# The small tasks of both batch halves in one slot between the large matmuls

## The chip, the cores and the metric

One NeuronCore of a Trainium2 chip runs one program. The metric is the device time of that program in microseconds; less is better. The kernel before takes 1516.54 us (median of three runs, 1514.53 to 1518.94).

## The reference

Three stages follow one another. Batch 4, 8 heads, 768 positions, head width 48; 3072 tokens of width 384.

```python
k_n = k / (norm(k) + 1e-06)                    # delta rule, one position after another
for t in range(S):
    y[t] = q[t] @ state
    v_old = state.T @ k_n[t]
    state = state + beta[t] * outer(k_n[t], v[t] - v_old)
p = domain_probs / (domain_probs.sum(-1) + 1e-09)
x1 = sum over 4 experts e of p[:, e] * (relu(x @ w1[e]) @ w2[e])      # 384 -> 1024 -> 384
out = (sigmoid(x1 @ w_gate) * (x1 @ w_val)) @ w_out                   # 384 -> 1536 -> 384
```

## The kernel before, in words

The delta rule is cut into 12 steps of 64 positions (`c` from 0 to 11). Within a step it becomes small matmuls and one triangular system per head, which VectorE solves by forward substitution ("inv"). Two steps give a block of 512 tokens, and the two MLP stages work on a block at a time. Each phase is one expert of one block (`m1`, 8 units) or the second MLP of one block (`m2`, 12 units). The first block's first expert is two phases of 256 tokens. In each unit `emit_a` (L689) makes the hidden part `ph` and `emit_b` (L726) multiplies it back into `acc`. Each product of float32 numbers is three passes over split operands (`xhi`, `xlo`, `hhi`, `hlo`, and the weights `ws`), so a large matmul has 512 columns and comes in threes. After `emit_a`, VectorE and ScalarE split the new hidden part; `emit_b` uses it two units later, and at the end of a phase all at once. At the end of the last expert's phase `finish` makes `xhi` and `xlo` of the second MLP out of `acc`, through VectorE and ScalarE.

The delta rule's work is laid between the large matmuls. The batch's four sequences sit two and two on the partitions, and `i` (0 or 1) says which half of the batch a task is for. `chain(c)` lists the rows of a step in the order of their dependence, each with a task for `i = 0` and one for `i = 1`:

- `ks` (`ks_task`, L499 and L500): keys times state into `pk`; VectorE then writes `R` = `V` - `pk`
- `half` (`half_task`, L512, steps 0 to 3 alone): two halves of the triangular solve; after the first ScalarE writes `U`, after the second VectorE writes `R`
- `tb` (`tb_task`, L521): the solved inverse `Xbd` times `R` into `pu`; VectorE writes `rhsA` and `rhsB`
- `y` (`y_task`, L534 and L535, for early steps L546): the outputs; ScalarE copies them out
- `s` (`s_task`, L571 and L572): the new state; ScalarE copies it into `rhsA` and `rhsB`

A `tb` or `half` task shows as 16 matmuls in the trace; `ks`, `y` and `s` as 32, 16 for each of their two lines. `plan_g` plans four Gram tasks a step (`g_task`, L318, 8 matmuls each in the trace), two heads' groups `hg` for each half `i`. The results of a task go into a PSUM bank of `at_p`, which has two.

The order of all this is written out by a planner when the program is built. `plan(t, fn, kind)` puts an item on the list `todo` with a planned time, in microseconds of large matmuls alone. The main loop counts such time in `now`, and calls `slot()` at fixed places: after each `emit_a`, after each `emit_b`, and inside each `emit_a` of the second MLP. A slot issues the items that are due, up to and with the first one of kind "pe". So one "pe" item goes into one slot. A step's rows lie `gap` apart (1.9 for step 1, 3.9 from step 2 on), and slots are about 1.94 apart (0.98 in the phases of 256 tokens). Work of VectorE that has time (the substitution, and the decoding of the second MLP's weights) is issued by `fill()` at these places. It goes by two counters: `pe_at`, the time that PE's work so far should have taken, and `vec_at` for VectorE. `fill` stops adding when `vec_at` is more than `SLACK` ahead of `pe_at`.

Of the kernel before, what the change touches and what calls it, by code (L numbers as in the profile page):

```python
# [84 lines left out]
def moe_delta_kernel(  # L85
# [17 lines left out]
    pe_at, vec_at = [0.0], [0.0]  # L103
# [176 lines left out]
    q = [nc.sync, None]  # L280

    def load_kq(c):
        (q[1] or q[0]).dma_start(out=KQ, in_=kq[c])

    def load_ks(c):
        (q[1] or q[0]).dma_start(out=KS, in_=kq[c, :, 0])

    def fill_bd(bd, t, i, eng):
        eng(out=bd[64:112, i, :, 0:C], in_=t[i][64:112, 0])
        eng(out=bd[0:48, i, :, C:P], in_=t[i][0:48, 0])  # L290

    def load_ys(c):
        if c:
            (q[1] or q[0]).dma_start(out=YQ[64:112, 0], in_=kq[c, 64:112, 1])
            (q[1] or q[0]).dma_start(out=YQ[0:C, 1], in_=kq[c, 0:C, 1])
        kv = kt[c].rearrange("p (i h d) -> p i h d", i=2, h=H)
        (q[1] or q[0]).dma_start(out=KI[0:C, 0], in_=kv[0:C])
        (q[1] or q[0]).dma_start(out=KI[C:P, 1], in_=kv[C:P])
        pd = pd_t.pop(c).rearrange("p (i h t) -> p i h t", i=2, h=H)
        q[0].dma_start(out=YQ[0:C, 0], in_=pd[0:C])  # L300
        q[0].dma_start(out=YQ[C:P, 1], in_=pd[C:P])

    def load_v(c):
        (q[1] or q[0]).dma_start(out=V.rearrange("p i h d -> p (i h d)"), in_=vt[c])
# [9 lines left out]
    def g_mm(i, hg, bd, kq_t):  # L314
        pg = bank([P, 4, 2, C], "pg")
        for j in range(4):
            h = hg * 4 + j
            nc.tensor.matmul(out=pg[:, j], lhsT=bd[0:112, i, h], rhs=kq_t[i][0:112, :, h], start=True, stop=True)  # L318
        return pg

    def g_l(pg, c, i, hg):
        hs = slice(hg * 4, hg * 4 + 4)
        vec.tensor_tensor(
            out=Lts[c % 2][:, i, hs],
            in0=pg[:, :, 0],
            in1=w_all[:, 2 * c + i, hs].unsqueeze(2).to_broadcast([P, 4, C]),
            op=ALU.mult,
        )

    def g_p(pg, c, i, hg):  # L330
        vec.tensor_tensor(
            out=Pts[c % 2][:, i, hg * 4 : hg * 4 + 4],
            in0=pg[:, :, 1],
            in1=mask_sb.unsqueeze(1).to_broadcast([P, 4, C]),
            op=ALU.mult,
        )
# [15 lines left out]
    def l_out(c):  # L352
        lt = Lts[c % 2]
        r, c2 = INV_OF[c]
        steps, small = INV[r]
        l_done.add(c)
        lv = [lt[o : o + HC].rearrange("p i h t -> p (i h) t") for o in range(0, P, HC)]
        if small:
            if c2 == 0:
                ld_t[r] = dr.tile([len(steps), 2, 2, H, 2, HC, HC], F32, tag=f"ls{len(steps)}", name="ls")  # L360
                od_t[r] = dr.tile([len(steps), 2, H, 2, HC, HC], F32, tag=f"lo{len(steps)}", name="lo")
            for a in range(2):
                for bp in range(2):
                    q[0].dma_start(
                        out=ld_t[r][c2, a, :, :, bp].rearrange("i h s t -> s (i h) t"),
                        in_=lv[2 * bp + a][:, :, a * HC : (a + 1) * HC],
                    )
            return
        if c2 == 0:
            ld_t[r] = dr.tile([len(steps), 2, H, 2, HC, 3 * HC], F32, tag="ld", name="ld")  # L370
        for bp in range(2):
            ld = ld_t[r][c2, :, :, bp]
            q[0].dma_start(out=ld[:, :, :, 0:C].rearrange("i h s t -> s (i h) t"), in_=lv[2 * bp])  # L373
            q[0].dma_start(
                out=ld[:, :, :, C:].rearrange("i h s t -> s (i h) t"), in_=lv[2 * bp + 1][:, :, HC:]
            )

    def l_off(c):
        lt = Lts[c % 2]
        r, c2 = INV_OF[c]  # L380
        if INV[r][1]:
            for bp in range(2):
                q[0].dma_start(
                    out=od_t[r][c2, :, :, bp].rearrange("i h s t -> s (i h) t"),
                    in_=lt[bp * C : bp * C + HC].rearrange("p i h t -> p (i h) t")[:, :, HC:],
                )

    def p_out(c):
        pd_t[c] = dr.tile([P, 2 * H * C], F32, tag=f"pd{c % 2}", name="pd")
        q[0].dma_start(out=pd_t[c], in_=Pts[c % 2].rearrange("p i h t -> p (i h t)"))  # L390
# [81 lines left out]
    def x_in(c):  # L472
        r, c2 = INV_OF[c]
        for bp in range(2):
            if INV[r][1]:
                for a in range(2):
                    put(Xbd, bp * C + a * HC, bp * C + a * HC, HC, xd_t[r][c2, a, :, :, bp])
            else:
                put(Xbd, bp * C, bp * C, C, xd_t[r][c2, :, :, bp])

    def off_in(c):
        r, c2 = INV_OF[c]
        if INV[r][1]:
            for bp in range(2):
                put(Ld, bp * C, bp * C + HC, HC, od_t[r][c2, :, :, bp])

    def scale_v(c):
        for i in range(2):
            nc.gpsimd.tensor_tensor(
                out=R[:, i] if c == 0 else V[:, i],  # L490
                in0=V[:, i],
                in1=nrm_all[:, 2 * c + i].unsqueeze(2).to_broadcast([P, H, D]),
                op=ALU.mult,
            )
# [100 lines left out]
    def chain(c):  # L595
        rows = [[lambda i=i: ks_task(c, i) for i in range(2)]] if c else []
        if INV[INV_OF[c][0]][1]:
            rows += [[lambda i=i, q=q: half_task(c, i, q) for i in range(2)] for q in range(2)]
        rows += [[lambda i=i: tb_task(c, i) for i in range(2)]]
        if c:  # L600
            rows += [[lambda i=i: y_task(c, i) for i in range(2)]]
            rows += [[lambda i=i: s_task(c, i) for i in range(2)]] if c < NC - 1 else []
        return rows
# [170 lines left out]
    def plan(t, fn, kind=""):  # L774
        todo.append((t, len(todo), kind, fn))
# [5 lines left out]
    def fill():  # L781
        while True:
            due = sorted((v[0][0], k) for k, v in back.items() if v and v[0][0] <= now[0])
            due = [(t, k) for t, k in due if len(back[k][0]) == 3 or back[k][0][3]()]
            now_ = [k for _, k in due if back[k][0][1] != "dve"]
            if not due or not now_ and vec_at[0] > pe_at[0] + SLACK:
                return
            ks = now_ or [k for _, k in due if k != turn_[0]] or [due[0][1]]
            if ks[0] == turn_[0] == "inv":
                vec_at[0] += SERIAL  # L790
            turn_[0] = ks[0]
            back[ks[0]].pop(0)[2]()

    def slot():
        fill()
        while todo and todo[0][0] <= now[0]:
            kind = todo[0][2]
            todo.pop(0)[3]()
            if kind == "pe":
                pe_at[0] += 1.7  # L800
                break
        fill()

# [27 lines left out]
    def plan_chain(c, t, gap):  # L831
        rows = chain(c)
        if c > 1:
            plan(t - 6.0, lambda: scale_v(c))
        if c > 1 and c % 2 == 0:

            def first():
                while inv_done[0] <= INV_OF[c][0]:
                    back["inv"].pop(0)[2]()
                x_in(c)  # L840
                off_in(c)

            plan(t - 8.0, first)
        for r, row in enumerate(rows):
            for q, fn in enumerate(row):
                plan(t + gap * (r + 0.5 * q), fn, "pe")
        t1 = t + gap * len(rows)
        if c % 2 == 0 and c:
            plan(t1 - 2 * gap, lambda: (x_in(c + 1), off_in(c + 1)))
        if c + 1 < NC:  # L850
            plan(t + 2 * gap, lambda: (load_v(c + 1), load_ks(c + 1)))
            plan(t1 + 3.0 if c > 1 else 75.0, lambda: load_ys(c + 1))
        return t1
# [9 lines left out]
    def plan_g(c, t):  # L863
        plan(t, lambda: load_kq(c))
        for i in range(2):
            plan(t + 12, lambda i=i: fill_bd(bdG, KQi, i, nc.scalar.copy))

        def g_task(i, hg):
            pg = g_mm(i, hg, bdG, KQi)
            g_l(pg, c, i, hg)  # L870
            g_p(pg, c, i, hg)

        for n, (i, hg) in enumerate([(0, 0), (0, 1), (1, 0), (1, 1)]):
            plan(t + 14 + 2 * n, lambda i=i, hg=hg: g_task(i, hg), "pe")
        plan(t + 23, lambda: (l_out(c), l_off(c), p_out(c)))

    def startup():
# [146 lines left out]
    with tc.manual_schedule():  # L1024
# [11 lines left out]
        for c in range(4, NC, 2):  # L1036
            t = dec_mem[c // 2] if c < NC - 2 else dec_mem[2]
# [121 lines left out]
```

## Time and profile before

| | us |
|---|---|
| median of three runs | 1516.54 (1514.53 to 1518.94) |
| profiled execution, its own time | 1512.61 |
| its span | 1510.8 |
| PE matmul busy | 1468.1 (97%) |
| PE weight load busy | 1222.8 (81%) |
| VectorE busy | 1066.9 (71%) |
| ScalarE busy | 574.4 (38%) |
| GpSimd busy | 264.9 (18%) |

Of the chain of work that ended last, PE has 86%, VectorE 8% and DMA 3%. Busy times overlap; a matmul's end is modelled and reaches into the next one, so distances are taken from start to start.

### The profile page before, as it was taken

What the parts mean: (1) busy time and instruction counts of PE and PEld (TensorE: products, weight loads), DVE (VectorE), ACT (ScalarE), POOL (GpSimd) and SP (SyncE); (2) the same over time, 40 slices, a digit from 0 to 9 for tenths busy, and PEclk for the clock granted to TensorE, in tenths of its full rate; (3) what the DMA queues carried; (4) which work ended last, traced back from release to release, by engine and by line L of the source; (5) the groups of instructions that cost most, each with busy time, mean ns of one, the idle gap of its engine ahead of it and who ended that gap; (6) DMA issues with size and microseconds to landing.
All of it is one profiled execution on the core that took longest, in us unless ns stands there. A gap on an engine that the chain in (4) does not pass through costs nothing.

```text
span 1510.8 us, 23046 instructions
## 1 busy us (share of the span) xinstructions
PE 1468.1 (97%) x8801; PEld 1222.8 (81%) x8801; DVE 1066.9 (71%) x1905; ACT 574.4 (38%) x921; POOL 264.9 (18%) x293
## 2 busy tenths in 40 slices
PE   5799899999999999999999999999999999999998
PEld 5688777888888888888888888888888888888887
DVE  8877998846888766778766778757778754444553
ACT  4045444533333334333343333343433343433343
POOL 4241457530011200012110002220001210001000
PEclk8689999999999999999999999999999999999999
DMA  8586688675443675444584435495433463333221
GB/s 231 163 260 208 222 267 266 215 202 151 150 139 109 181 189 146 140 141 128 162 208 133 133 116 165 132 225 144 133 102 106 132 163 94 123 101 108 88 94 63
DMA packets 97749, 235.50 MB, mean 156 GB/s; under 512 B 23544, under 2 KB 29816, under 8 KB 95608
## 3 DMA queue, kind: packets, MB, share of 16 engines
q1 hardware_dynamic: 87352, 195.04, 43.2%
q0 software_dynamic: 10144, 38.94, 9.9%
q8 instruction: 69, 1.13, 0.3%
q14 instruction: 40, 0.33, 0.1%
q10 hardware_dynamic: 144, 0.07, 0.0%
HBM read 202.10 MB, written 27.97 MB: 152 GB/s over the span
## 4 chain that ended last, share of the span: by engine, by line
PE 86%; DVE 8%; DMA 3%; issue 2%; ACT 1%; SPq 0%; DVEq 0%; ACTq 0%
PE ph L689 43%; PE acc L726 33%; PE pu L521 3%; PE pg L318 2%; DVE Xpp L112 1%; DVE itmp L112 1%; PE pk L499 1%; PE ps L571 1%; DMA raw<-in_wp 1%; DVE ws L112 1%; DMA ls<-LP 1%; PE yt L534 1%; DVE hlo L112 1%; PE pu L512 1%; PE yt L535 1%
## 5 line engine op out<-in xcount | busy, mean ns | idle before, releaser
L689 PE MATMUL ph<-xhi,ws 128*128 128x512 f32 (+1 forms) x2064 | 635.4, 390 | 1.5 <-ACT xhi L756 0.8
L726 PE MATMUL acc<-hhi,ws 128*128 128x512 f32 (+1 forms) x1632 | 497.2, 387 | 0.0
L689 PEld LDWEIGHTS ph<-xhi,ws 128*128 128x128 f32 x2064 | 378.4, 188 | 77.2 <-ACT xhi L589 1.3
L689 PE MATMUL ph<-xlo,ws 128*128 128x512 f32 (+1 forms) x1032 | 398.2, 386 | 0.7 <-DVE xlo L112 0.7
L726 PEld LDWEIGHTS acc<-hhi,ws 128*128 128x128 f32 x1632 | 302.0, 189 | 59.3 <-ACT hhi L696 0.3
L112 DVE TENSOR_TENSOR ws<-raw,ws 128x768 fp32r<-128x768 f32 x308 | 298.3, 970 | 60.8 <-ACT ws L190 58.1
L726 PE MATMUL acc<-hlo,ws 128*128 128x512 f32 (+1 forms) x816 | 314.5, 385 | 8.3 <-DVE hlo L112 8.2
L190 ACT CAST ws<-raw 128x768 fp32r<-128x768 f32 x308 | 253.8, 830 | 83.5 <-PE acc L726 63.8
L696 ACT ACTIVATE hhi<-ph 128x512 fp32r<-128x512 f32 (+1 forms) x200 | 116.2, 581 | 418.6 <-PE ph L689 410.9
L689 PEld LDWEIGHTS ph<-xlo,ws 128*128 128x128 f32 x1032 | 194.2, 188 | 41.8 <-DVE xlo L112 2.6
L112 DVE SCALAR_TENSOR_TENSOR hlo<-ph,hhi 128x512 fp32r<-128x512 f32 (+1 forms) x200 | 132.6, 666 | 130.6 <-ACT hhi L696 130.5
L726 PEld LDWEIGHTS acc<-hlo,ws 128*128 128x128 f32 x816 | 154.0, 189 | 40.6 <-DVE hlo L112 10.2
L112 DVE TENSOR_TENSOR itmp<-Xpp,Lpp 128x120 f32<-128x120 f32 (+27 forms) x403 | 174.3, 445 | 9.7 <-DMA Lpp<-ls 3.8
L112 DVE TENSOR_TENSOR Xpp<-Xpp,itmp 128x120 f32<-128x120 f32 (+27 forms) x403 | 176.2, 449 | 5.1
L112 DVE TENSOR_TENSOR gv<-ph,sg 128x512 f32<-128x512 f32 x72 | 49.7, 691 | 94.7 <-PE ph L689 94.6
L705 ACT CAST hhi<-gv 128x512 fp32r<-128x512 f32 x72 | 44.6, 620 | 171.7 <-DVE gv L112 171.7
L753 POOL TENSOR_TENSOR ACC<-ACC,ctmp 128x512 f32<-128x512 f32 x36 | 50.1, 1393 | 321.1 <-DVE ctmp L112 320.5
L112 DVE TENSOR_TENSOR hlo<-gv,hhi 128x512 fp32r<-128x512 f32 x72 | 51.3, 713 | 49.4 <-ACT hhi L705 49.4
L703 ACT ACTIVATE sg<-ph 128x512 f32<-128x512 f32 x72 | 43.0, 597 | 76.7 <-PE ph L689 76.7
L373 POOL DMA_DIRECT2D ld<-LP x16 | 10.7, 670 | 333.5 <-DVE LP L112 333.5
L318 PE MATMUL pg<-KQ,bdG 112*128 112x128 f32 x320 | 45.2, 291 | 15.1 <-ACT bdG L290 10.8
L318 PEld LDWEIGHTS pg<-KQ,bdG 112*128 112x128 f32 x320 | 43.6, 205 | 20.0 <-ACT bdG L290 12.4
(163 smaller groups left out, 1104.7 us busy)
## 6 DMA issues: line engine op xcount, KB each, us to landing
raw<-in_wp SPq DMA_DIRECT2D x200, 384.0 KB, 3.1
raw<-w_d SPq DMA_DIRECT2D x108, 384.0 KB, 3.5
KQ<-in_kq SPq DMA_DIRECT2D x9, 896.0 KB, 7.9
pd<-LP POOLq DMA_DIRECT2D x12, 512.0 KB, 8.1
YQ<-pd POOLq DMA_DIRECT2D x24, 256.0 KB, 7.0
Lpp<-ld POOLq DMA_DIRECT2D x8, 768.0 KB, 13.5
pe<-p_d SPq DMA_DIRECT2D x23, 256.0 KB, 4.4
dec_a<-in_wp SPq DMA_DIRECT2D x15, 384.0 KB, 4.3
```

What stands on the lines that cost most here:

```text
L112: return fn(*args, **kw)
L190: nc.scalar.copy(out=w[:, 0], in_=t)
L318: nc.tensor.matmul(out=pg[:, j], lhsT=bd[0:112, i, h], rhs=kq_t[i][0:112, :, h], start=True, stop=True)
L499: nc.tensor.matmul(out=pk[0:C, h], lhsT=KS[C:112, i, h], rhs=rhsA[C:112, i, h], start=True, stop=True)
L512: nc.tensor.matmul(out=pu[0:m, h], lhsT=lhsT, rhs=rhs, start=True, stop=True)
L521: nc.tensor.matmul(out=pu[:, h], lhsT=Xbd[:, i, h], rhs=R[:, i, h], start=True, stop=True)
L689: nc.tensor.matmul(out=res[q], lhsT=lt, rhs=rt, start=(k == 0 and j == 0), stop=(k == KT - 1 and j == 2))
L696: nc.scalar.activation(out=hh, in_=res[0], func=AF.Relu)
L703: nc.scalar.activation(out=sg, in_=res[0], func=AF.Sigmoid)
L705: nc.scalar.copy(out=hh, in_=gv)
L726: nc.tensor.matmul(out=acc_t[d][:, :w], lhsT=lt, rhs=rt, start=(u == 0 and j == 0), stop=(u == nf - 1 and j == 2),)
L753: (nc.vector if e == NE - 1 else nc.gpsimd).tensor_tensor(out=a, in0=a, in1=t, op=ALU.add)
```

## The change

`plan_chain` plans one "pe" item for a whole row, which calls the tasks of both halves one after the other; before, the second was an item of its own, half a gap later. `plan_g` plans two items a step, each with the two Gram tasks of one half, 4 apart; before, there were four, 2 apart. In `slot` every "pe" item now adds 3.4 to `pe_at`, not 1.7. This holds as well for the four items that remain single tasks: `s` of step 0 and the transposes of step 1, two each.

```diff
             if kind == "pe":
-                pe_at[0] += 1.7
+                pe_at[0] += 3.4
                 break
...
         for r, row in enumerate(rows):
-            for q, fn in enumerate(row):
-                plan(t + gap * (r + 0.5 * q), fn, "pe")
+            plan(t + gap * r, lambda row=row: [fn() for fn in row], "pe")
...
-        for n, (i, hg) in enumerate([(0, 0), (0, 1), (1, 0), (1, 1)]):
-            plan(t + 14 + 2 * n, lambda i=i, hg=hg: g_task(i, hg), "pe")
+        for i in range(2):
+            plan(t + 14 + 4 * i, lambda i=i: [g_task(i, hg) for hg in range(2)], "pe")
```

## Rows read from the trace of the kernel before

**Rows 1.** The page, slices of the span: granted TensorE clock in tenths
```profile
PEclk8689999999999999999999999999999999999999
```
**Rows 2.** Stretches, PE alone: stretch, its length, PE busy (count), PEclk, DMA share, GB/s
```profile
49.70:80.40 30.70, 26.56 (x167) 0.50 0.61 191
107.70:118.00 10.30, 10.30 (x66) 0.50 0.90 304
186.30:189.70 3.40, 3.40 (x9) 0.51 0.98 340
300.00:1430.00 1130.00, 1130.00 (x6707) 1.00 0.50 142
```
**Rows 3.** Timeline of PE: start, us, line, out<-in, count, [idle before, releaser]
```profile
185.55 0.50 PE L726 MATMUL acc<-hlo,ws 128*128 128x512 f32 x1 [4.25 <-DVE hlo L112]
...
228.59 0.50 PE L726 MATMUL acc<-hlo,ws 128*128 128x512 f32 x1 [2.24 <-DVE hlo L112]
```
**Rows 4.** Timeline of PE around an s task and a ks task
```profile
534.68 0.39 PE L689 MATMUL ph<-xlo,ws 128*128 128x512 f32 x1
535.00 0.24 PE L571 MATMUL ps<-rhsA,KI 112*48 112x48 f32 x1
...
536.42 0.40 PE L726 MATMUL acc<-hlo,ws 128*128 128x512 f32 x1
...
537.11 0.39 PE L726 MATMUL acc<-hlo,ws 128*128 128x512 f32 x1
...
747.29 0.39 PE L726 MATMUL acc<-hlo,ws 128*128 128x512 f32 x1
...
749.24 0.40 PE L689 MATMUL ph<-xlo,ws 128*128 128x512 f32 x1
```
**Rows 5.** Timeline of PE around a Gram task and a tb task
```profile
429.31 0.40 PE L726 MATMUL acc<-hlo,ws 128*128 128x512 f32 x1
...
430.91 0.39 PE L689 MATMUL ph<-xlo,ws 128*128 128x512 f32 x1
...
520.18 0.39 PE L689 MATMUL ph<-xlo,ws 128*128 128x512 f32 x1
...
522.66 0.40 PE L689 MATMUL ph<-xlo,ws 128*128 128x512 f32 x1
```
**Rows 6.** Timeline of PE in the startup: two half tasks side by side
```profile
51.36 5.33 PE L512 MATMUL pu<-R,Xbd 128*96 128x48 f32 x32 [4.64 <-POOL LP L345]
```
**Rows 7.** Groups of PE instructions by line: count | busy us, mean ns | idle before
```profile
L499 PE MATMUL pk<-rhsA,KS 48*64 48x48 f32 x352 | 24.8, 220 | 0.0
L534 PE MATMUL yt<-YQ,rhsA 112*64 112x64 f32 x320 | 21.3, 229 | 0.0
L571 PE MATMUL ps<-rhsA,KI 112*48 112x48 f32 x352 | 20.2, 210 | 0.0
```
**Rows 8.** Timeline: start of ks, then VectorE's R, at steps 2, 6, 10
```profile
266.18 0.25 PE L499 MATMUL pk<-rhsA,KS 48*64 48x48 f32 x1
272.91 0.55 DVE L112 TENSOR_TENSOR R<-V,pk 128x384 f32<-128x384 f32 x1
...
747.61 0.25 PE L499 MATMUL pk<-rhsA,KS 48*64 48x48 f32 x1
753.34 0.55 DVE L112 TENSOR_TENSOR R<-V,pk 128x384 f32<-128x384 f32 x1
...
1207.85 0.25 PE L499 MATMUL pk<-rhsA,KS 48*64 48x48 f32 x1
1212.93 0.55 DVE L112 TENSOR_TENSOR R<-V,pk 128x384 f32<-128x384 f32 x1
```
**Rows 9.** Waits of PE after 129.4: us in total, times, longest
```profile
PE pu L512 <- DVE R L112: 0.6, 1, 0.6
```
**Rows 10.** Timeline in the first phase: VectorE's R for half, PE's wait before tb
```profile
92.96 1.00 DVE L112 TENSOR_TENSOR R<-V,pk 128x384 f32<-128x384 f32 x2
106.73 2.75 PE L521 MATMUL pu<-R,Xbd 128*128 128x48 f32 x16 [2.32 <-DVE R L112]
```

## The prediction

> **What bounds the kernel now.** I read the page's clock line first. TensorE runs at its lower level only in a few stretches of the first 190 us and at full clock from there to the end [rows 1, 2]. The stretch table then shows PE busy for 1130.00 of the 1130 us from 300 to 1430 [rows 2]. In that stretch a microsecond of PE work removed is a microsecond of the kernel, and any new wait of PE is added in full. Before 245 us it is otherwise: VectorE's queue is behind, and PE waits for it twice at the end of a phase, 4.25 us before 185.55 and 2.24 us before 228.59 [rows 3]. There PE time saved is mostly given back. What a small task costs PE beyond its own matmuls is read from the timeline around one visit, and how late VectorE answers from its timeline.
>
> **The change part by part.**
>
> *Joining two tasks in a slot.* The last large matmul before an `s` task starts at 534.68, the third one after it at 536.42: 1.74 us [rows 4]. Three large matmuls in a row take 0.69 us (536.42 to 537.11), so a visit costs 1.05 us. Inside the task a pair of matmuls comes every 0.045 us, and 16 pairs are 0.72 us. The other 0.33 us is the price of going into the task and out of it. For `ks` the same sum is 749.24 - 747.29 - 0.69 = 1.26 us against 16 pairs of 0.058 us, again 0.33 us [rows 4]. `y`, of the same build, is taken at 0.33 us too. For `tb` it is different: 522.66 - 520.18 - 0.69 = 1.79 us, and its 16 matmuls need about 0.11 us each, so almost nothing is lost at the edges [rows 5]. A Gram task (`pg`) is the same: 430.91 - 429.31 - 0.69 = 0.91 us for 8 matmuls of 0.11 us [rows 5]. I cost joining `tb`, both kinds of `half` and `pg` at zero.
>
> Does a second task join on without a gap? The trace has one such place. In the startup two `half` tasks stand side by side as one piece of 32 in 5.33 us, at half clock [rows 6], which leaves no room for a break. So a joined pair saves the whole 0.33 us; bounds 0 (each task pays its edge as now) and 0.36. The counts of L499, L571 and L534 [rows 7], divided by 16, are 22 `ks`, 22 `s` and 20 `y` tasks: 11 pairs of `ks`, 10 of `s` (the two of step 0 stay apart), 10 of `y` and one in the older form. Of these 32 pairs three fall into the first phase, below. 29 x 0.33 = 9.6 us less.
>
> The row shows an edge. The Trainium skill ("TensorE: Matmul & The Clock Gate", Part 2, step by step) says the opposite: PE pulls weight loads ahead of matmuls in flight, so that the next weights load under the running matmul. By that rule alone an edge would cost nothing and joining would save 0 instead of 9.6 us. For `tb` and `pg` the trace agrees (0.0 us); for `ks` and `s` it measures 0.33 us, and I go by the rows.
>
> *Earlier tasks wait at the start of an even chain.* Adding up the planned times, I get the same slots for the first task of nearly every row. But `ks` of steps 2, 4, 6, 8, 10 stands at the end of an expert phase, and the next row came two slots later, after 18 large matmuls and the second `ks`. Now it comes in the slot inside the first `emit_a` of the second MLP, after 12. From the first `ks` matmul that is two tasks of 0.93 us, 0.25 us of way out and 12 x 0.23 us: 4.9 us. The row needs `R`, which VectorE writes only after the finishing work of the phase in its queue, at a time that does not depend on the slots. At step 6 `ks` starts at 747.61, PE is ready at 752.5, and `R` is done at 753.34 + 0.55 + 0.06 = 753.95: a wait of 1.4 us. At step 10 it is 1212.7 against 1213.54, 0.8 us [rows 8]; steps 4 and 8, read the same way, give 0.4 and 0.9. At step 2 it is 271.1 against 273.5, 2.4 us, of which 0.6 us is waited for already [rows 8, 9]. Together 0.4 + 1.4 + 0.9 + 0.8 + 1.8 = 5.3 us more. Behind a waiting `tb` stand only the six large matmuls of that `emit_a`; nothing else is due sooner. Bounds: 0 if VectorE reaches `R` earlier, 9 if all five wait as step 2 does.
>
> Odd chains have at least nine large matmuls between dependent rows, over 3 us from a first task's end to the row that needs it. The PSUM banks alternate as before. The evacuations of a pair are queued together, so the second one's comes earlier than today. I cost this at nothing.
>
> *The first phase (82.5 to 129.4 us).* Chain 1 has one row per 1.9 us of plan. Today its 16 tasks do not fit the 14 slots, and `tb` waits 2.32 us for `R`, which stands in VectorE's queue behind the norms of steps 4 to 11 [rows 10]. With pairs the second `half` row is issued two slots earlier, ahead of the norms, so this wait goes (-2.3). In its place the first `half` row comes 1.4 us before `R` (written at 92.96 [rows 10]), and `y` about 1.4 us before the `rhs` products that now stand behind the norms (+2.8). Three pairs save 1.0; one task fewer hangs over into the next phase (-0.4). The half-clock stretch from 107.7 [rows 2] followed the wait of `tb` and cost about 4.3 us; I give two chances in three that it goes (-2.8). Sum -3.7; bounds -6 and +5 (the clock falls after the long `half` pairs and stays low).
>
> *The book-keeping.* Every "pe" entry now adds 3.4 to the planner's clock, also the four that stay single. The filler for VectorE may then be issued up to 10 us of plan earlier in the first two phases. It is the same filler, and VectorE is the limit there till 245 us, so I cost it at zero; bounds -2 and +3. The Gram pairs of steps 4 and 5 lie in that stretch: zero too.
>
> *The clock.* A `tb` pair keeps PE on small matmuls for 3.5 us where it was 1.8. In the startup PE ran `half` tasks without a break from 51.36 on, and the grant was 0.50 throughout [rows 2, 6]: these matmuls did not bring the clock back. Of the three long waits after 100 us, two were followed by a fall (at 107.7 and 186.3) and one, that before 228.59, was not [rows 2, 3]. In the fall at 186.3 PE got 9 large matmuls into 3.40 us [rows 2], where 0.23 us each would be 15: a fall costs 6 x 0.23 = 1.4 us. There will be 11 `tb` pairs and three of the second `half`, five of them or their neighbours with a wait in front. None falling is one bound, all of them (14 x 1.4 = 20 us) the other. I take two, where wait and pair stand together: +2.8 us.
>
> **Sum.** -9.6 + 5.3 - 3.7 + 2.8 = -5.2 us on the profiled execution of 1512.61 us (span 1510.8): 1507.4. The median shown, 1516.54, is 3.9 us above that execution; the same sum on it gives 1511.3, and that is the forecast.
>
> **The rivals.**
> - *The clock holds.* No new fall, and the low stretch of the first phase goes: -9.6 + 5.3 - 5.2 = -9.5, or 1507. For it: one of three waits passed without a fall. Against: the other two.
> - *The waits eat the gain.* The chain starts all cost what step 2 does, or one of the 1.4 us waits is longer by VectorE's backlog: -9.6 + 9 - 0.5 = -1, or 1515.5. For it: `R` came 5.4 and more us after its matmuls at steps 2 and 6. Against: it is read from an order in the queue that stays.
> - *Slower: the clock falls after the pairs.* Place: `tb` pairs in the second MLP's phases. Price 1.4 us each. With a first phase that wins nothing it decides from the fourth fall on (-9.6 + 5.3 + 5.6 = +1.3); nine give +8.3, or 1525. For it: the grant of 0.50 beside unbroken `half` matmuls. Against: large matmuls at full rate stand on both sides.
> - *No edge to save.* PE hides the switch, and what the rows show as edge is only moved: 0 + 5.3 - 2.7 + 2.8 = +5.4, or 1522. That is what the Trainium skill's rule named above ("TensorE: Matmul & The Clock Gate") would make of it. Against: 0.33 us in every visit, and none in `tb`.
>
> **How the numbers follow.** Forecast 0.47 (own range 1507.5 to 1515), clock holds 0.22, waits eat it 0.17, clock falls 0.10, no edge 0.04. 0.3% is 4.5 us, about what can be told from no change, so faster means under 1512.0. The forecast's range straddles that: a little over half of it and nearly all of the second case make faster 0.51; same 0.36; slower 0.13. The range for 8 in 10 takes in the second and third cases and the near part of the fourth: 1502 to 1521.
>
> **What would show it.** The timeline at a `ks`, `s` or `y` pair: 64 matmuls in one piece, no gap in the middle, and a third large matmul after it at 0.33 us less than two visits. At the five even chain starts a wait of PE for `R` of 0.4 to 2.4 us. In the first phase no 2.3 us wait before `tb`. The clock line and the stretches of `tb` pairs: falls or none. The forecast is wrong if the pair has a gap in its middle, if the clock falls more than four times after 245 us, or if the waits for `R` exceed 7 us in sum.

## The result, and the profile after

The changed kernel takes 1526.39 us (median, 1521.23 to 1533.47), the kernel before beside it 1514.44 (1511.71 to 1518.94): a ratio of 1.0074, interval 1.0052 to 1.0096. By the ratio the change makes the kernel slower by about 11 us. The third rival, "the clock falls after the pairs", has nearly this time (1525), but it got there by nine falls of 1.4 us each, and the trace shows five that cost twice as much: that its number fits is luck.

The profiled execution has 1521.86 us, a span of 1520.1, so 9.3 more than the span of before. It is one of the shorter runs: timed runs of the changed kernel go from 1521.23 us at a mean clock of 0.973 to 1533.47 at 0.961. What follows explains the 9.3 us that the two traces show; the rest of the difference is taken up under "Open".

First the stretches of the changed kernel with PE alone: stretch, its length, PE busy (count), PEclk, DMA share, GB/s. PE is TensorE, DVE VectorE and ACT ScalarE; PEclk is the granted clock as a share of full speed. They answer to [rows 2].

```profile
102.30:105.70 3.40, 3.40 (x18) 0.50 1.04 287
184.20:191.00 6.80, 5.28 (x12) 0.50 0.99 290
228.60:232.00 3.40, 2.85 (x7) 0.50 1.04 373
276.40:283.20 6.80, 6.80 (x27) 0.50 0.78 261
525.50:532.40 6.90, 6.90 (x25) 0.51 1.04 232
761.00:767.90 6.90, 6.90 (x24) 0.51 1.01 222
996.60:1003.40 6.80, 6.80 (x26) 0.50 0.95 205
1225.30:1228.70 3.40, 3.40 (x13) 0.50 0.96 322
```

The last five are new: one at the start of each of the even steps 2, 4, 6, 8, 10, and none anywhere else after 245 us. Before, full clock ran unbroken there. In the timeline of PE at step 4 (start, us, operation, count, idle before it) one sees what precedes a fall, and then an odd step's `tb` pair for comparison:

```profile
521.98 0.39 PE L689 MATMUL ph<-xlo,ws 128*128 128x512 f32 x1
523.23 4.95 PE L521 MATMUL pu<-R,Xbd 128*128 128x48 f32 x32 [0.87 <-DMA Xbd<-xd]
527.97 1.20 PE L689 MATMUL ph<-xhi,ws 128*128 128x512 f32 x2
528.97 0.63 PE L689 MATMUL ph<-xlo,ws 128*128 128x512 f32 x1
...
568.21 0.39 PE L689 MATMUL ph<-xlo,ws 128*128 128x512 f32 x1
568.43 3.67 PE L521 MATMUL pu<-R,Xbd 128*128 128x48 f32 x32
571.92 0.71 PE L689 MATMUL ph<-xhi,ws 128*128 128x512 f32 x2
```

At step 4 PE idles 0.87 us, then runs the pair; the granted clock goes to half within it (525.5), and the three large matmuls behind it, which take 0.69 us at full clock, take 1.43 (527.97 to 529.40, where the next three begin). At step 5 nothing is waited for, the pair takes 3.49 us from start to start and the large matmuls go on at full rate.

PE's waits after 82 us (line waited for, us, times, longest):

```profile
PE acc L726 <- DVE hlo L112: 9.9, 4, 6.1
PE pu L512 <- DVE R L112: 3.4, 2, 2.2
PE pu L521 <- DVE R L112: 2.1, 3, 1.3
PE acc L726 <- DVE ws L112: 1.6, 2, 0.8
...
PE pu L521 <- DMA Xbd<-xd: 0.9, 1, 0.9
```

To place the 9.3 us I compare the start of the same large matmul in both traces, just ahead of each group of tasks and a dozen large matmuls behind it:

| stretch | after minus before, us |
|---|---|
| up to the end of the first phase (131 us) | -3.1 |
| 131 to 265 us | +4.5 |
| steps 2, 4, 6, 8, 10 | +3.5, +3.2, +2.6, +3.6, +0.9: +13.8 |
| steps 3, 5, 7, 9, 11 | -1.25, -1.17, -1.17, -1.17, -0.81: -5.6 |
| Gram pairs after 245 us | -0.4 |

The odd steps gain what the joined pairs were to gain; the even ones lose far more than their waits; and what the first phase gained is gone before 265 us. (The changed kernel is 1.1 us late already ahead of the first phase.)

### The profile page after: what moved, and what is told of

It reads as the page before. It is cut to its first block, busy times and chain, and to the rows that moved or that the text cites. A ratio compares the mean times of both kernels' runs of the same rounds, so it can differ in the third digit from the quotient of the medians.

```text
span 1520.1 us, 23049 instructions
## 1 busy us (share of the span) xinstructions
PE 1470.7 (97%) x8801; PEld 1234.3 (81%) x8801; DVE 1062.7 (70%) x1905; ACT 574.9 (38%) x921; POOL 269.9 (18%) x293
## 4 chain that ended last, share of the span: by engine, by line
PE 83%; DVE 9%; DMA 3%; issue 2%; ACT 2%; SPq 0%; POOL 0%; DVEq 0%; ACTq 0%
PE ph L689 42%; PE acc L726 31%; PE pu L521 3%; PE pg L318 2%; DVE Xpp L112 2%; DVE ws L112 1%; PE pu L512 1%; DVE itmp L112 1%; DMA ls<-LP 1%; DVE hlo L112 1%; PE ps L571 1%; PE yt L534 1%; DVE ACC L753 1%; DVE ctmp L112 1%; ACT xhi L756 1%
## 5 line engine op out<-in xcount | busy, mean ns | idle before, releaser
L689 PEld LDWEIGHTS ph<-xhi,ws 128*128 128x128 f32 x2064 | 385.7, 191 | 80.2 <-ACT xhi L589 1.3
L726 PEld LDWEIGHTS acc<-hlo,ws 128*128 128x128 f32 x816 | 154.8, 190 | 41.6 <-DVE hlo L112 11.4
L521 PEld LDWEIGHTS pu<-R,Xbd 128*128 128x128 f32 x384 | 52.2, 219 | 7.9 <-DVE R L112 7.3
L521 PE MATMUL pu<-R,Xbd 128*128 128x48 f32 x384 | 52.4, 301 | 5.1 <-DVE R L112 4.3
```

The costliest lines, as they stand in the source:

```text
L521: nc.tensor.matmul(out=pu[:, h], lhsT=Xbd[:, i, h], rhs=R[:, i, h], start=True, stop=True)
L689: nc.tensor.matmul(out=res[q], lhsT=lt, rhs=rt, start=(k == 0 and j == 0), stop=(k == KT - 1 and j == 2))
L726: nc.tensor.matmul(out=acc_t[d][:, :w], lhsT=lt, rhs=rt, start=(u == 0 and j == 0), stop=(u == nf - 1 and j == 2),)
```

## The experiments

The theories. **A**: a wait of PE ahead of a `tb` or `half` pair makes the clock fall, and that is the loss. **B**: the waits cost their own length, and the clock is an accident. **C**: the long pair does it by itself. **D**: the wait does it by itself, or the place at an expert's end. **E**: the loss is made before 245 us. Ratios are to the kernel before, timed on the same chip beside each run (medians 1515.2 to 1515.9). "Half clock" is the time at half clock between 245 us and the last matmul in the profiled execution (30.8 us in the changed kernel); "chains" is the sum of the distances of steps 2 to 11 as in the table above (+8.2 there).

**1. The row behind `ks` one slot later at even steps.**

```diff
-            plan(t + gap * r, lambda row=row: [fn() for fn in row], "pe")
+            late = 1.0 if c % 2 == 0 and r == 1 else 0.0
+            plan(t + gap * r + late, lambda row=row: [fn() for fn in row], "pe")
```

> The changed kernel, but in the even steps from 2 on the row after ks is planned 1.0 later, so that it comes in the next slot and R is there when PE reaches it. Pairs stay pairs. Theory A (the clock falls where PE waits for R and then runs a tb or half pair; the pair alone does not do it): no fall after 260 us, each of the five even chains takes 1 to 2 us less than in the kernel before instead of 0.9 to 3.6 more; 1526 - 19 = about 1508. Rival B (the waits cost by themselves, the clock is a side effect): only the waits go, 1526 - 5 = 1521. Rival C (a tb pair alone lowers the clock, and even chains are only where it hit): falls stay, 1521 to 1526.

Measured: 1511.59 us, ratio 0.9982 (0.9966 to 0.9999). Half clock 10.3 us, all of it at step 2, where the `tb` pair now waits 1.8 us; from 312 us on PE runs at full clock throughout:

```profile
299.51 5.97 PE L521 MATMUL pu<-R,Xbd 128*128 128x48 f32 x32 [1.84 <-DVE R L112]
```

```profile
312.00:1480.00 1168.00, 1167.12 (x6947) 1.00 0.49 142
```

The even steps 4 to 10 turn from +10.3 in sum to -3.7, steps 2 to 11 from +8.2 to -4.0. The waits of those four steps were 3.0 us in all; putting them away puts the falls away, and 14 us come back: B falls. (The profiled execution, 1520.38 us, is the longest of the twelve; it loses its time before 265 us, where it has 27.3 us at half clock in the first phase, and nothing above rests on that part.)

**2. `tb` and `half` in single tasks again, with the waits left in.** An item of kind "pe1" takes a slot too, and adds 1.7 to `pe_at`; so in the runs below.

```diff
+            if 0 < r < len(rows) - (2 if c < NC - 1 else 1):
+                for q, fn in enumerate(row):
+                    plan(t + gap * (r + 0.5 * q), fn, "pe1")
+                continue
             plan(t + gap * r, lambda row=row: [fn() for fn in row], "pe")
...
```

> The changed kernel, but tb and half tasks go one to a slot as in the kernel before; ks, y, s and Gram tasks stay in pairs. The first tb of an even chain still comes in the slot inside the first emit_a and waits for R. Theory A (wait and pair together): no fall after 260 us at steps 4 to 10, 1526 - 13 = about 1513. Rival C (the long pair alone): the same. Rival D (the wait alone is enough): falls stay at the even chains, about 1525.

Measured: 1511.93 us, ratio 0.9983 (0.9960 to 1.0006). The timeline shows the waits that are left, at steps 4, 8 and 10:

```profile
522.19 1.99 PE L521 MATMUL pu<-R,Xbd 128*128 128x48 f32 x16 [0.56 <-DVE R L112]
...
986.25 1.99 PE L521 MATMUL pu<-R,Xbd 128*128 128x48 f32 x16 [0.63 <-DVE R L112]
...
1211.28 1.99 PE L521 MATMUL pu<-R,Xbd 128*128 128x48 f32 x16 [0.85 <-DVE R L112]
```

None of the three is followed by a fall. Half clock is 3.4 us, at step 2, where a single `half` task stands behind a wait of 2.17 us; chains -4.0. So in these three places a wait under 0.9 us with a single task behind it did not lower the clock, and the longer wait of step 2 did.

**3. Large matmuls put into the wait.** Ten at step 2 and six at each later even step, on old operands into a spare bank; their results are not used.

```diff
...
+            if c % 2 == 0 and r == 1:
+                row = [lambda: large(10 if c == 2 else 6)] + row
```

> The changed kernel with large matmuls added whose result nobody reads: ten before the row after ks at step 2, six at steps 4, 6, 8 and 10, in all 34 (7.7 us at full clock). They lie where PE waits for R. Theory A: PE has more to do and the kernel is faster all the same, because the clock stays up: no fall at the even chains after 260 us, about 1516. Rival B (the clock is a side effect): 2 us slower than the changed kernel, about 1528. Rival C: falls stay, 1526 to 1528.

Measured: 1516.07 us, ratio 0.9994 (0.9975 to 1.0013). No half clock after 245 us; chains -4.7, the even steps between -0.1 and +0.4 though they carry 1.4 to 2.3 us of useless work each. With 34 large matmuls more than in the changed kernel, these steps end sooner. PE from 300 us on:

```profile
300.00:1480.00 1180.00, 1179.24 (x6993) 1.00 0.49 141
```

The same stretch of the changed kernel holds 6938 matmuls, at a mean clock of 0.99. The pair is the same, the place is the same, and the wait is filled: no fall.

**4. Pairs from step 2 on, all before 245 us as before.** Step 1, its neighbours and the Gram tasks of steps 4 and 5 are single again.

```diff
+            if c == 1:
+                for q, fn in enumerate(row):
+                    plan(t + gap * (r + 0.5 * q), fn, "pe1")
+                continue
             plan(t + gap * r, lambda row=row: [fn() for fn in row], "pe")
...
```

> The changed kernel with everything up to 245 us issued as in the kernel before: chain 1 and the Gram tasks of steps 4 and 5 one task to a slot, 1.7 counted for each single task. Pairs from step 2 on. Theory A: the loss is made at the even chains after 260 us, so this is about as slow as the changed kernel: 1514 + 13.8 - 5.2 = 1523. Rival E (it is lost before 245 us, through the planner's counter and VectorE's backlog): about 1512.

Measured: 1523.6 us, ratio 1.0048 (1.0030 to 1.0065). Most of the loss stays (1.0048 of 1.0074), so most of it is made after 245 us, and E falls as the account of the whole. Half clock 34.0 us, chains +10.5. But step 4's pair waited and did not fall, and two falls stand at odd steps, 3 and 5. The one at step 5 follows a pair that waited for nothing:

```profile
524.55 3.77 PE L521 MATMUL pu<-R,Xbd 128*128 128x48 f32 x32 [0.95 <-DVE R L112]
...
566.53 3.77 PE L521 MATMUL pu<-R,Xbd 128*128 128x48 f32 x32
570.08 1.20 PE L689 MATMUL ph<-xhi,ws 128*128 128x512 f32 x2
571.08 0.63 PE L689 MATMUL ph<-xlo,ws 128*128 128x512 f32 x1
```

The pair of step 5 (566.53) ran at full rate; the large matmuls behind it start at half clock. So C holds sometimes, and A is a tendency, not a law.

**5. The same with the later row.** Run 4 and run 1 together.

> All before 245 us as in the kernel before, pairs from step 2 on, and at even steps the row after ks one slot later. Theory A (a wait in front of a tb or half pair makes the clock fall): no half-clock stretch at the starts of steps 4, 6, 8, 10, and each of those chains, like the odd ones, takes 0.5 to 1.4 us less than in the kernel before: about -9 us in all, 1506 to 1509 if the kernel before has 1515. Rival C (the long pair by itself can lose the clock, wait or not): at least two of the nine chains 3 to 11 still have a stretch of 3.4 us or more and stand 1 to 3 us over the others; then -2 to -5 us. Rival E (the gain is lost before 245 us and nothing depends on the chains): as the kernel before.

Measured: 1513.13 us, ratio 0.9990 (0.9975 to 1.0005); this misses the expected 1506 to 1509. Steps 4 to 11 are as expected (-0.5 to -1.3 each, no fall), but steps 2 and 3 have half clock, 10.2 and 3.4 us, and cost +6.2. At step 2 the row after the two `half` pairs is late now:

```profile
288.65 6.40 PE L521 MATMUL pu<-R,Xbd 128*128 128x48 f32 x32 [2.23 <-DVE R L112]
```

At step 3 the fall follows a `tb` pair that waited for nothing; in run 4 it was the second `half` pair there, which had not waited either. So the pairs of these two steps, three rows of them one after another, can be followed by a fall without a wait too.

**6. The same with `tb` and `half` apart.** Only `ks`, `y` and `s` are pairs.

```diff
+            if 0 < r < len(rows) - (2 if c < NC - 1 else 1):
+                for q, fn in enumerate(row):
+                    plan(t + gap * (r + 0.5 * q) + late * (1 - q), fn, "pe1")
+                continue
...
```

> As the run before it, but the tb and half tasks stay apart, one in a slot; only ks, y and s are pairs (30 pairs less the ones of step 1). If the 0.33 us edges are real and tb pairs save nothing, each chain from 3 on takes 0.5 to 1.2 us less than in the kernel before and no chain from 3 on has a half-clock stretch: -8 to -11 us, 1504 to 1507 if the kernel before has 1515. Rival C's cause is gone here, so if falls at chains remain, the pairs of tb are not what makes them.

Measured: 1511.4 us, ratio 0.9969 (0.9957 to 0.9980): faster than before, but short of the expected 1504 to 1507. No half clock after 245 us; chains -5.8, odd steps -1.1, -0.8 for the last. The even steps 4 to 10 gain nothing (-0.2 to +0.2) where 0.5 to 1.2 us was expected: the second `tb` now comes late, and `y` waits behind it at each of them, 0.7 us (`yt`, for ScalarE's `YT`).

**7. The reverse: pairs in step 1 and the Gram tasks of steps 4 and 5 alone.**

```diff
+            if c > 1:
+                for q, fn in enumerate(row):
+                    plan(t + gap * (r + 0.5 * q), fn, "pe1")
+                continue
             plan(t + gap * r, lambda row=row: [fn() for fn in row], "pe")
...
```

> The reverse of pairs from step 2: pairs only in step 1 and in the Gram tasks of steps 4 and 5, all later work as in the kernel before. The prediction's term for the first phase (-3.7 us, carried to the end): 1511 if the kernel before has 1515. Theory G (VectorE sets the time up to 245 us, so what PE saves in the first phase comes back as waits before 245 us): the gain of 2 to 6 us at 131 us is gone by 245 us, and the time is within 1.5 us of the kernel before, 1514 to 1517.

Measured: 1516.72 us, ratio 1.0017 (1.0002 to 1.0031). The first phase gains 3.8 us from its own start, and at the end of the next expert's phase PE waits longer for VectorE:

```profile
187.52 0.80 PE L726 MATMUL acc<-hlo,ws 128*128 128x512 f32 x1 [6.10 <-DVE hlo L112]
```

It was 4.25 us [rows 3]. From the first phase's end to 265 us the kernel loses 2.3 us of it again; the other 1.5 us are less than executions differ there (see "The first phase" below). What decides is the timed runs: the median is 1.3 us above the kernel before, so no gain of the size of the prediction's 3.7 us reaches the end.

**8. A wait made at odd steps.** Run 1, and at odd steps from 3 on `ks` and the row behind it in one item, so that the row has to wait for `R` where it never did.

```diff
+            if c % 2 and c > 1:
+                if r == 1:
+                    continue
+                if r == 0:
+                    row = row + rows[1]
...
```

> As the run with the later row at even steps, but at the odd steps 3, 5, 7, 9, 11 the ks pair and the row after it are one item, so that tb (half at step 3) has to wait for R right after ks, some 0.5 to 1.5 us. Theory A: the clock falls after that wait at most of the five odd chains, where neither the kernel before nor the changed one has a fall; each such chain is 2 to 4 us longer than with the later row, 10 to 18 us in all, so 1522 to 1530. Rival D (the place matters, the end of an expert's phase, not wait and pair): the wait costs its own length, 0.5 to 1.5 us a chain, no fall, 1514 to 1519.

Measured: 1524.41 us, ratio 1.0071 (1.0045 to 1.0096). Steps 5, 7 and 9 wait 0.89, 2.40 and 0.89 us, and each falls; step 11, the last line of the first four below, waits for nothing:

```profile
563.09 6.60 PE L521 MATMUL pu<-R,Xbd 128*128 128x48 f32 x32 [0.89 <-DVE R L112]
...
801.84 6.44 PE L521 MATMUL pu<-R,Xbd 128*128 128x48 f32 x32 [2.40 <-DVE R L112]
...
1038.96 4.79 PE L521 MATMUL pu<-R,Xbd 128*128 128x48 f32 x32 [0.89 <-DVE R L112]
...
1266.10 3.77 PE L521 MATMUL pu<-R,Xbd 128*128 128x48 f32 x32
```

```profile
563.60:573.90 10.30, 10.30 (x41) 0.50 0.02 8
802.60:812.80 10.20, 10.20 (x38) 0.50 0.02 7
1041.50:1048.30 6.80, 6.80 (x23) 0.50 0.00 0
```

They turn from -1.17 to +4.6, +6.1 and +3.0 us. Steps 3 and 11, whose pairs turned out to wait for nothing, do not fall, though `ks` stands right ahead of them too; so it is not the longer run of small tasks alone. (Step 2 has the fall of run 1 again, 6.8 us behind a wait of 1.83.) The expectation held at the three places where there was a wait. The end of an expert's phase is not needed for a fall, and neither are transfers: DMA is nearly still in these stretches, and nearly full in those of the changed kernel.

**9. The best of it.** Run 5, with the `half` and `tb` rows of steps 2 and 3 single.

```diff
+            late = 1.0 if c % 2 == 0 and r == 1 else 0.0
+            if c < 4 and 0 < r < len(rows) - 2:
+                for q, fn in enumerate(row):
+                    plan(t + gap * (r + 0.5 * q) + late * (1 - q), fn, "pe1")
+                continue
...
```

> All before 245 us as in the kernel before; at steps 2 and 3 the half and tb tasks stay apart; every other row of steps 2 to 11 is a pair, and at even steps the row after ks comes one slot later. Theory A with C for the half pairs (a wait in front of a tb pair, or the pairs of half, make the clock fall; tb pairs without a wait from step 4 on do not): no half-clock stretch after 245 us, steps 2 and 3 0.4 to 1.2 us less, the even steps 4 to 10 0.5 to 1.3 us less each, the odd ones 1.17 (0.81 for the last): -9 to -10 us, 1504 to 1507 if the kernel before has 1515. Rival C in full (any tb pair can lose the clock): one to three stretches of 3.4 us or more at steps 4 to 11, each 1.4 us or more, 1507 to 1512.

Measured: 1505.9 us (1504.22 to 1510.35), ratio 0.9942 (0.9926 to 0.9958): 9 us faster than the kernel before. No half clock after 245 us, every one of the ten steps shorter (-0.5 to -1.2), chains -10.0:

```profile
245.00:1480.00 1235.00, 1233.12 (x7342) 1.00 0.49 145
```

**10. The wait at odd steps, with a single `tb` behind it.** Run 8, but only the first task of the row is in the item with `ks`.

```diff
                 if r == 1:
-                    continue
+                    row = row[1:]
                 if r == 0:
-                    row = row + rows[1]
+                    row = row + rows[1][:1]
```

> As the run with ks and tb in one item at odd steps, but only the first task of that row is in the item; the second comes in the slot of the row. So PE waits for R at the odd chains as it did there (1 to 2.4 us at steps 5, 7, 9), but a single tb follows, not a pair. Theory A (wait and pair together): no half-clock stretch at steps 5, 7, 9; each of them longer than with the later row by its wait alone, 0.5 to 2.5 us; 1513 to 1518. Rival D (the wait alone does it): stretches at steps 5, 7, 9 as there, 1520 to 1527.

Measured: 1521.49 us (1511.07 to 1525.12), ratio 1.0031 (1.0014 to 1.0049). The median is in rival D's range, though less than run 8. In the profiled execution, one of its shortest at 1514.18 us, steps 5, 7 and 9 go three ways:

```profile
557.52 3.65 PE L521 MATMUL pu<-R,Xbd 128*128 128x48 f32 x16 [2.53 <-DVE R L112]
...
793.35 1.99 PE L521 MATMUL pu<-R,Xbd 128*128 128x48 f32 x16 [1.41 <-DVE R L112]
...
1027.93 1.99 PE L521 MATMUL pu<-R,Xbd 128*128 128x48 f32 x16 [0.89 <-DVE R L112]
```

Half clock of 6.8 us goes with the first, 3.5 us follows the second, none the third. The first begins at 556.7, still within the wait, before any `tb` matmul. With step 2 of run 2 that makes three falls without a pair, at waits of 1.41, 2.17 and 2.53 us: there D holds, and what A expected of run 10 missed. In run 10 the `ks` pair stands right ahead of the wait, in run 2 large matmuls do, so the two do not give one limit. Nor does a long wait always do it: ahead of a large matmul at 228.6 to 233.0 us [rows 3] PE waited 1.44 to 2.52 us in the kernel before and in runs 4, 5, 6 and 9, and the clock held in all five traces.

**All `tb` tasks of steps 4 to 11 together**, over the profiled executions of the changed kernel and of runs 1 to 5 and 8 to 10 (singles without a wait, as in all of runs 6 and 7, are left out; none of them was followed by a fall):

| in front of it, and what follows | followed by half clock |
|---|---|
| wait of 0.21 to 2.40 us, then a pair (changed kernel, runs 4 and 8) | 10 of 11 |
| no wait, a pair (changed kernel, runs 1, 3 to 5, 8 to 10) | 1 of 49 |
| wait of 0.56 to 0.89 us, then a single (runs 2 and 10) | 0 of 4 |
| wait of 1.41 and 2.53 us, then a single (run 10) | 2 of 2 |

The pairs of the earlier steps are not in this table, and they are less clear. At steps 2 and 3, six pairs behind waits of 1.83 to 2.28 us were all followed by a fall, four behind 0.13 to 0.18 us were not, and of 31 without a wait two were (runs 4 and 5). In the first phase the first `half` pair waited 1.25 to 1.27 us in six traces with the same order of work there, and the clock fell within it in three of them (runs 1, 7 and 8; not in runs 3 and 10, and in the changed kernel only at 102.3, behind the second `half` pair, which had waited for nothing):

```profile
94.65 2.92 PE L512 MATMUL pu<-R,Xbd 128*96 128x48 f32 x32 [1.26 <-DVE R L112]
```

```profile
94.66 4.25 PE L512 MATMUL pu<-R,Xbd 128*96 128x48 f32 x32 [1.25 <-DVE R L112]
```

The first line is the changed kernel's, the second run 1's.

## Why the prediction was wrong

**Joining saves the edge: right.** The `ks` pair of step 4, PE's timeline:

```profile
517.03 0.39 PE L726 MATMUL acc<-hlo,ws 128*128 128x512 f32 x1
517.35 0.25 PE L499 MATMUL pk<-rhsA,KS 48*64 48x48 f32 x1
...
519.20 0.22 PE L500 MATMUL pk<-rhsB,KS 48*64 48x48 f32 x1
...
519.92 0.40 PE L689 MATMUL ph<-xlo,ws 128*128 128x512 f32 x1
```

64 matmuls in one piece; 519.92 - 517.03 - 0.69 = 2.20 us, where two visits are 2.52: 0.32 us saved for 0.33 predicted. The odd steps 3 to 9 have three such pairs each, 1.0 us predicted, 1.17 to 1.25 measured. Gram pairs gain 0.4 us in all, as good as the zero predicted. The tasks with an edge are those whose lines show 48*64, 112*64 or 112*48 [rows 4, 7]; `tb` shows 128*128 like the large matmuls, and the Gram tasks 112*128. Whether that makes the edge was not tested. The rule weighed against this (the Trainium skill, "TensorE: Matmul & The Clock Gate", Part 2, step by step) would, taken without the conditions that the page sets for it, have given 0; the trace measures 0.32 us for these tasks.

**The waits at even steps: right in sum.** 2.17, 0.87, 0.63, 1.29 and 0.21 us, less the 0.6 of before, are 4.6 us for 5.3 predicted. One by one they were up to 0.8 us off (2.4, 0.4, 1.4, 0.9 and 0.8 forecast), so that the sum is this close is partly luck. In four of the five it is `R`; step 4's is put down to `Xbd`'s transfer, which came last there.

**The clock: the step that failed.** "I take two, where wait and pair stand together: +2.8 us" named the right coincidence and then did not count its places. By the prediction's own list there were five of them, and all five fell; more than four was its own sign of being wrong. The size was off as well: 1.4 us a fall was read from a low stretch of 3.4 us [rows 2], and four of the five were 6.8 or 6.9 long. The even steps lost 13.8 us; without their waits (+4.6) and edges (-5.0, at the 0.33 us of the prediction) that leaves 14.2 us for the falls, 2.8 each, where the sum had 2.8 in all. For 30.8 us at half clock that is 0.46 us lost per us; the prediction's 1.4 for 3.4 us is 0.41, so the price per us was nearly right, and the number of falls and their length were not. Runs 1 and 3 take the wait from the pair at steps 4 to 10 and the falls go; run 8 makes waits elsewhere and falls appear. The rival had the mechanism but not the condition: it spoke of "nine" falls after pairs wherever they are, and gave it one chance in ten.

**The first phase: the sum carried a gain that could not be carried.** Of the mechanism most came: the 2.3 us wait ahead of `tb` is gone, the first `half` row waits 1.26 us (1.4 forecast), and half clock is 3.4 us long instead of 10.3; but the 1.4 us wait of `y` did not come (0.28). The phase gains 4.2 us from its own start, 3.7 predicted; in this execution, for the same order of work gave from -5.4 to +6.3 us here in the traces of runs 1, 3, 8 and 10, with 0 to 27.3 us at half clock, so the closeness is luck. And the first paragraph of the prediction said that PE time saved before 245 us is mostly given back, and the sum did not follow it. The end of the next phase waits for VectorE at the same place of its queue:

```profile
185.72 0.80 PE L726 MATMUL acc<-hlo,ws 128*128 128x512 f32 x1 [6.12 <-DVE hlo L112]
...
225.57 0.70 PE L726 MATMUL acc<-hhi,ws 128*128 128x512 f32 x2 [0.74 <-DVE ws L112]
...
229.15 0.80 PE L726 MATMUL acc<-hlo,ws 128*128 128x512 f32 x1 [2.10 <-DVE hlo L112]
```

185.55 there before, 185.72 now. There is a wait for `ws` besides, a fall of 6.8 us for 3.4 and one more at 228.6. The longer fall is not shown to come of the longer wait: with the wait of before, runs 4, 5 and 9 have 6.8 or 6.9 us there too. That this stretch costs more is no accident of one execution: from 131 to 265 us the changed kernel and runs 1, 3, 8 and 10, which issue the same work there, lose 2.3 to 5.1 us against the kernel before, and runs 4, 5, 6 and 9, with the order of before, only 0.2 to 0.9. Net at 265 us: +1.4 us, of which 1.1 already stands ahead of the first phase.

**The sum.** Predicted -5.2, measured +9.3: the falls are 11.4 us more than their term, the first phase with what follows it 5.1 more, the waits 0.7 less, the odd steps and the Gram pairs 1.3 better.

**Open.** The timed runs of the changed kernel lie up to 12 us above its profiled execution, at a lower mean clock; which falls those runs had more of is in no trace of theirs. The first phase is one place for it: run 1's profiled execution, with the same work there, stands 12.1 us behind the kernel before at 265 us, where the changed kernel's stands 1.4. Why one pair of 49 fell without a wait, why one of 11 did not fall with one, and why the first phase's pair fell in three traces of six, was not settled. Nor was the book-keeping of 3.4 tried by itself.

## What to carry to other kernels

When tasks of small matmuls are joined, put the joined piece where nothing is waited for: read the wait ahead of each one, and where there is one give it a slot more, or, where the wait is short, leave that task single. Price a fall of the clock by its time at half clock (here 14.2 us for 30.8), not by the shortest stretch in the trace, and count it at every place that meets the condition, not at some of them. And where another engine sets the time of a stretch, enter what PE saves in it as zero in the sum, not only in the words.

## What was not expected of the hardware

A wait of 0.21 us ahead of a `tb` pair (step 10) was followed by 3.4 us at the lower clock level (0.50, which is 1.2 of 2.4 GHz), while single tasks behind waits of 0.56 to 0.89 us kept the full one (four places), and so did the second `half` pair of step 2 behind 0.13 to 0.18 us (runs 1, 5, 8 and 10). And more work took less time: 34 useless large matmuls in the waits (run 3) brought the ratio to the kernel before from 1.0074 (1.0052 to 1.0096) to 0.9994 (0.9975 to 1.0013).
